# Chunk loads of the first blocks moved into free places of a weight matrix, in a retention kernel with two dense layers

## The chip, the cores and the metric

The kernel runs on one core of a Trainium2 chip. The metric is the device time of one launch in microseconds (us). PE is TensorE, DVE is VectorE, ACT is ScalarE, POOL is GpSimd, SP is the engine whose queue issues nearly all transfers (DMAs).

## The reference

What is computed, shortened (B 4, H 8, S 576, D 64; 2304 tokens, model width 512, hidden width 2048, all in float32):

```python
scores = (1 / sqrt(D)) * q @ k.T                       # per batch and head
Dmat   = where(i >= j, gamma[h] ** (i - j), 0)
x      = ((scores * Dmat) @ v)                         # to [2304, 512]
h      = x @ w_in;  x = (h * cos(h)) @ w_out           # first layer
h      = x @ w_in2                                     # second layer
g      = where(h >= 1, h, where(h <= -1, 0, (h + 1) ** 2 / 4))
out    = g @ w_out2
```

The weights arrive as float64; the kernel takes their words apart and makes of each a pair of float32r numbers (a high and a low part).

## The kernel before

The 2304 tokens are cut into five blocks of 256, 512, 512, 512 and 512 tokens, and a block into chunks of at most 128 tokens of one batch. The first two blocks have seven chunks, called c0 to c6 here (c0 and c1 in the first block, c2 to c6 in the second; c4 and c6 have 64 tokens). The third block has four, called k0 to k3.

**Retention.** A chunk is a `Chunk` object. `load` brings three tensors: `qk` (512 KB), `kv` (512 KB) and `pt`, a table of powers (256 KB for 128 tokens). `prep` multiplies v by a table of powers (one DVE instruction). `scores` puts k times q into two PSUM banks, `masked` multiplies them by the causal mask into the tile R (two DVE instructions), `full` adds the state T times q and forms the new state, `inner` multiplies by R, `state` updates T, and `post` scales the result into `xhl`, the block's input for the first layer as a high and a low part (one ACT and two DVE instructions).

**First layer.** A slot (l, c) is block l with hidden chunk c of 16: `mm1` (12 matmuls into a bank h), then `actA`, `actB`, `actC` on ACT, DVE and POOL (h times cosine, split into `gh` and `gl`), and two slots later `mm2` (12 matmuls into the block's banks). The first two blocks share their weights while these are converted: `slots` interleaves (0, c) with (1, c), block 0 ahead by LEAD. A converted `wi` tile lives in the pool `wr` from its use by (0, c) to its use by (1, c) and is also written to memory (`wd`), to be read again for the later blocks (`load_wi`). The converted `w_out` tiles stay in the places `wo0` to `wo15` of the pool `wp`. Each weight chunk is loaded by `load_raw` into a conversion buffer (`raw` or `rsh` of the pool `cv`, two of each), and `begin` and `convert` work on it with buffers X, W and C of the same pool. From the third slot on, the conversions wait for the last `post` of the first two blocks (`after=lastpost`).

**Second layer.** It starts when the first is done with all blocks; its weights are converted during blocks 2 to 4.

**What sets the order.** The program is written in the order shown, and a list of positions (`plan`, two positions for each slot) places the third block's chunks in the last slots of the second. The tile framework then orders the instructions of every engine by its own timeline and places each tile in its pool; a tile's next user waits until the last one is done. Every engine runs its queue in order. Before, the chunks' `qk` and `kv` share one tile of 16 KB per partition, from the pool `ap` (two places) for even chunks and from `xp` for odd ones. A chunk is asked for when the third before it is done.

Of the kernel before, what the change touches and what calls it, by code (L numbers as in the profile page):

```python
# [7 lines left out]
F32 = mybir.dt.float32  # L8
# [5 lines left out]
AF = mybir.ActivationFunctionType  # L14
# [4 lines left out]
B, H, S, D = 4, 8, 576, 64  # L19
NT, DM, DFF = B * S, H * D, 2048  # L20
P = 128
KB = DM // P
NP = H // 2
NC = DFF // P
# [8 lines left out]
SEQ = {p: k for k, (p, _, _) in enumerate(PRODS)}  # L33
LAG2 = 3
LAG = 2
LEAD = 2
TWICE = 4
MAGIC = 1.5 * 2.0 ** 23
INV2PI = 0.15915494309189535
# [26 lines left out]
def retention_moe_kernel(ctx: ExitStack, tc: tile.TileContext, qk, kv, win1, wout1, win2, wout2, mask, vtab, ptab, out):  # L66
    nc = tc.nc
    V, A, G, SY, PE = nc.vector, nc.scalar, nc.gpsimd, nc.sync, nc.tensor

    const = ctx.enter_context(tc.tile_pool(name="const", bufs=1))  # L70
    wp = ctx.enter_context(tc.tile_pool(name="wp", bufs=1))
    wr = ctx.enter_context(tc.tile_pool(name="wr", bufs=LEAD + 3))
    xp = ctx.enter_context(tc.tile_pool(name="xp", bufs=5))
    ap = ctx.enter_context(tc.tile_pool(name="ap", bufs=2))
    act = ctx.enter_context(tc.tile_pool(name="act", bufs=2))
    stp = ctx.enter_context(tc.tile_pool(name="stp", bufs=4))
    cv = ctx.enter_context(tc.tile_pool(name="cv", bufs=2))
# [83 lines left out]
    wi, wo = {}, {}  # L161
# [80 lines left out]
    CH = {}  # L242
# [8 lines left out]
    class Chunk:  # L251
# [6 lines left out]
            self.first, self.last = self.t == 0, self.t + self.n == S  # L258
            self.banks = banks

        def load(self, other=None, pool=None):
            n = self.n
            both = (pool or ap).tile([P, 4, DM], F32, tag="x" if pool else "qkv", name="qkv")
            self.qk = both[:, 0:2].rearrange("p a (i m) -> p a i m", i=NP)
            self.kv = both[:, 2:4]
            SY.dma_start(out=self.qk, in_=qk[self.i])
            (other or SY).dma_start(out=self.kv[:n], in_=kv[self.i][:n])
            self.pt = ap.tile([P, NP, P], F32, tag="pt", name="pt")
            (other or SY).dma_start(out=self.pt[:, :, :n], in_=ptab[:, :, self.t:self.t + n])

        def prep(self):
            n = self.n
            v = self.kv[:n, 1, :].rearrange("p (h d) -> p h d", h=H)
            V.tensor_tensor(out=v, in0=v, in1=vtb[:n, self.i, :].unsqueeze(2).to_broadcast([n, H, D]), op=ALU.mult)

        def scores(self):
# [4 lines left out]
                    js = slice(j * D, (j + 1) * D)  # L281
                    self.lastpe = PE.matmul(self.Z[j][:n, p * P:p * P + n], self.qk[js, 1, p, :n], self.qk[js, 0, p, :n], start=True, stop=True)

        def masked(self):
            n = self.n
            R = ap.tile([P, 2, NP, P], F32, tag="R", name="R", bufs=1)
            for j in range(2):
                V.tensor_tensor(
                    out=R[:n, j, :, :n], in0=self.Z[j][:n].rearrange("p (i m) -> p i m", i=NP)[:, :, :n],
                    in1=msk[:n, :n].unsqueeze(1).to_broadcast([n, NP, n]), op=ALU.mult)  # L290
            self.R = R

# [46 lines left out]


    slots = []
    for i in range(NC + LEAD):
        if i < NC:
            slots.append((0, i))
        if i >= LEAD:
            slots.append((1, i - LEAD))
    for l in range(2, NBLK):
        slots += [(l, c) for c in range(NC)]
    N1 = len(slots)
# [222 lines left out]
    for l in range(2, NBLK):  # L572
        s0, s1 = window[l]
        span = 2 * (s1 - s0) / len(members[l])
        for k, i in enumerate(members[l]):
            g = int(2 * s0 + k * span)
            e = int(2 * s0 + (k + 1) * span) - 1
            e = max(e, g)
            pos = [g, g + (e - g) // 3, e]
            ends[i] = e  # L580
            gl_ = max(g - 9, ends.get(i - 2, -99))

            banks = (("S", "O"), ("S", "O"), ("y0", "y1"), ("S", "O"))[k] if l == 2 else ("S", "O")

            def mk(i=i, g=g, pos=pos, gl_=gl_, banks=banks):
                def ld():
                    CH[i] = Chunk(i, banks)
                    CH[i].load()
                at(gl_, ld)
                at(g - 1, lambda: CH[i].prep())  # L590
                at(pos[0], lambda: CH[i].scores())
                at(pos[0], lambda: CH[i].masked())
                at(pos[1], lambda: CH[i].full())
                at(pos[1], lambda: CH[i].inner())
                at(pos[1], lambda: CH[i].state())
                at(pos[2], lambda: CH[i].post())
            mk()
# [18 lines left out]
    def first_load(k):  # L616
        i = first[k]
        CH[i] = Chunk(i, (("S", "O"), ("y0", "y1"), ("y2", "y3"))[k % 3])
        if k == 0:
            A.dma_start(out=vtb, in_=vtab)  # L620
            CH[i].load(A)
            A.dma_start(out=msk, in_=mask)
        else:
            CH[i].load(pool=xp if k % 2 else None)

    first_load(0)
    first_load(1)
    load_raw(0, 0, 0)
    first_load(2)
    load_raw(0, 1, 0)  # L630
    CH[first[0]].prep()
    for k, i in enumerate(first):
        c = CH[i]
        c.scores()
        c.masked()
        if k < 2:
            warm(10, c.lastpe)
        if k + 1 < len(first):
            CH[first[k + 1]].prep()
        c.full()  # L640
        c.inner()
        c.state()
        if k < 2:
            warm(10, c.lastpe)
        lastpost = c.post()
        if k + 3 < len(first):
            first_load(k + 3)
        if k == 2:
            make_wi1(0, begin(0, 0, 0))
            load_raw(0, 0, 1)  # L650
        if k == 4:
            make_wo1(0, begin(0, 1, 0))
            load_raw(0, 1, 1)
# [170 lines left out]
```

## Time and profile before

| | us |
|---|---|
| median of three runs (918.47 to 923.39) | 921.04 |
| the profiled execution | 920.45 |
| its span, first to last instruction | 918.6 |
| PE busy, share of the span | 876.8 (95%) |
| DVE busy, share of the span | 635.6 (69%) |
| ACT busy, share of the span | 474.4 (52%) |

A stretch in which PE is busy for its whole length can only be shortened by less work or a higher clock; a stretch in which it is not shows what PE waits for. The granted TensorE clock (PEclk) is given as a share of 2.4 GHz; 0.50 is 1.2 GHz. "A:B" is a stretch in us from the start of the span, "x12" a count of instructions, and "[3.60 <-DMA ...]" the idle time of the engine just before a row and what ended it.

### The profile page before, as it was taken

How to read it: one execution, taken by the hardware profiler on the slowest of the kernel's cores; microseconds unless marked ns; L12 is line 12 of the kernel's file. 1: busy time of each engine (PE TensorE's matmuls, PEld its weight loads, DVE VectorE, ACT ScalarE, POOL GpSimd, SP SyncE). 2: the span in 40 equal slices, each digit the busy share in tenths (PEclk: the TensorE clock that was granted, in tenths of full speed). 3: DMA queues.
4: the chain of work that ended last, by engine and by line, in shares of the span. 5: the costliest groups of instructions: out<-in, count | busy, mean ns of one | idle time of the engine just before them, and what ended most of it. 6: DMA issues, size and time to landing. Idle time of an engine off the chain costs nothing. (4 is left out here: it accounts for less than half of the span.)

```text
span 918.6 us, 13546 instructions
## 1 busy us (share of the span) xinstructions
PE 876.8 (95%) x4876; PEld 752.1 (82%) x4876; DVE 635.6 (69%) x1157; ACT 474.4 (52%) x885; POOL 104.5 (11%) x82
## 2 busy tenths in 40 slices
PE   7878899987999999999999989999899999999997
PEld 6767788876878777788888778888788989889896
DVE  5789899635686786887799787456754556655454
ACT  2348888833565665565677653334433334433332
POOL 0003232300111222222222200000000000000000
PEclk9879999998999999999999999999999999999999
DMA  9869889445487869585976897565575656665531
GB/s 341 274 220 337 292 315 312 161 155 178 161 300 228 307 237 317 178 293 174 322 281 240 296 368 240 178 195 168 201 271 176 190 182 202 221 209 171 166 96 70
DMA packets 78115, 211.81 MB, mean 231 GB/s; under 512 B 9696, under 2 KB 21728, under 8 KB 78048
## 3 DMA queue, kind: packets, MB, share of 16 engines
q1 hardware_dynamic: 77088, 210.01, 68.7%
q10 hardware_dynamic: 960, 0.93, 0.3%
q8 instruction: 39, 0.64, 0.3%
q14 instruction: 28, 0.23, 0.1%
HBM read 170.02 MB, written 40.89 MB: 230 GB/s over the span
## 5 line engine op out<-in xcount | busy, mean ns | idle before, releaser
L493 PE MATMUL hq<-xc,wq 128*128 128x384 f32 x1008 | 200.6, 337 | 5.3 <-ACT sX L508 4.8
L362 PE MATMUL h<-xhl,wi 128*128 128x512 f32 (+1 forms) x864 | 195.5, 374 | 3.7 <-ACT wi L158 2.4
L493 PEld LDWEIGHTS hq<-xc,wq 128*128 128x128 f32 x1008 | 180.1, 188 | 18.9 <-ACT sX L508 5.6
L362 PEld LDWEIGHTS h<-xhl,wi 128*128 128x128 f32 x864 | 151.0, 192 | 32.4 <-ACT wi L158 2.7
L425 POOL TENSOR_TENSOR gl<-t,gh 128x512 fp32r<-128x512 f32 (+1 forms) x78 | 104.3, 1340 | 427.8 <-ACT gh L424 389.5
L424 ACT ACTIVATE gh<-t 128x384 fp32r<-128x384 f32 (+2 forms) x176 | 95.9, 548 | 49.7 <-DVE t L528 27.9
L527 ACT ACTIVATE t<-t,half 128x384 f32<-128x384 f32 x96 | 59.0, 616 | 120.3 <-DVE t L526 120.2
L377 PE MATMUL bky<-gh,wo 128*128 128x512 f32 x256 | 102.6, 401 | 4.1 <-ACT gh L424 4.0
L378 PE MATMUL bky<-gh,wo 128*128 128x512 f32 x256 | 101.2, 395 | 0.0
L379 PE MATMUL bky<-gl,wo 128*128 128x512 f32 x256 | 87.7, 393 | 0.0
L528 DVE TENSOR_TENSOR t<-t,sC 128x384 f32<-128x384 f32 x96 | 53.3, 557 | 35.7 <-ACT t L527 35.7
L545 PE MATMUL bky<-wo,gh 128*128 128x512 f32 x192 | 75.7, 394 | 0.9 <-ACT gh L424 0.9
L546 PE MATMUL bky<-wo,gh 128*128 128x512 f32 x192 | 75.6, 394 | 0.0
L417 ACT ACTIVATE t<-t 128x512 f32<-128x512 f32 (+1 forms) x80 | 46.7, 586 | 52.8 <-DVE t L412 52.4
L425 DVE TENSOR_TENSOR gl<-t,gh 128x384 fp32r<-128x384 f32 (+1 forms) x98 | 54.4, 556 | 19.3 <-ACT gh L424 19.3
L526 DVE TENSOR_SCALAR t<-sC 128x384 f32<-128x384 f32 x96 | 34.3, 358 | 41.5 <-ACT sC L513 40.1
L377 PEld LDWEIGHTS bky<-gh,wo 128*128 128x128 f32 x256 | 48.8, 191 | 16.1 <-ACT gh L424 5.8
L547 PE MATMUL bky<-wo,gl 128*128 128x512 f32 x192 | 61.1, 394 | 0.0
L378 PEld LDWEIGHTS bky<-gh,wo 128*128 128x128 f32 x256 | 48.9, 191 | 9.9 <-issue 0.3
L379 PEld LDWEIGHTS bky<-gl,wo 128*128 128x128 f32 x256 | 48.0, 190 | 10.7 <-POOL gl L425 0.6
L142 DVE SCALAR_TENSOR_TENSOR W<-raw,X 128x512 int32<-128x512 int32 x64 | 52.5, 823 | 1.1
L134 ACT ACTIVATE X<-raw 128x512 f32<-128x512 f32 x64 | 42.3, 663 | 16.5 <-DMA raw<-in_win_dram 11.1
(126 smaller groups left out, 1368.5 us busy)
## 6 DMA issues: line engine op xcount, KB each, us to landing
wq<-wq SPq DMA_DIRECT2D x72, 512.0 KB, 4.1
wi<-wd SPq DMA_DIRECT2D x48, 512.0 KB, 5.0
wo<-wd SPq DMA_DIRECT2D x48, 512.0 KB, 4.6
raw<-in_win_dram SPq DMA_DIRECT2D x32, 512.0 KB, 6.0
raw<-in_wout_dram SPq DMA_DIRECT2D x32, 512.0 KB, 5.7
qkv<-in_qk_dram SPq DMA_DIRECT2D x20, 512.0 KB, 4.5
wd<-wi SPq DMA_DIRECT2D x16, 512.0 KB, 5.2
wd<-cw SPq DMA_DIRECT2D x16, 512.0 KB, 5.7
```

The lines of the kernel that those rows point to most:

```text
L362: PE.matmul(hp[s][:, :n], w[:, a, kb, :], x[b][:, kb, :], start=(i == 0), stop=(i == 3 * KB - 1))
L377: PE.matmul(o, w[:, 0, es], a, start=first and e % per == 0, stop=False, skip_group_check=True)
L378: PE.matmul(o, w[:, 1, es], a, start=False, stop=False, skip_group_check=True)
L379: PE.matmul(o, w[:, 0, es], b, start=False, stop=last, skip_group_check=True)
L424: A.activation(a, u, AF.Copy)
L425: eng.tensor_tensor(out=b, in0=u, in1=f(a), op=ALU.subtract)
L493: PE.matmul(o, w[:, a, kb, :], x[b][:, kb, :], start=first and i == 0, stop=i == 5, skip_group_check=True)
L527: A.activation(t, t, AF.Square, scale=0.5, bias=half)
L528: V.tensor_tensor(out=t, in0=t, in1=h, op=ALU.max)
L545: PE.matmul(y, a[:, js], w[:, 0, :], start=n == 0, stop=False)
L546: PE.matmul(y, a[:, js], w[:, 1, :], start=False, stop=False)
L547: PE.matmul(y, b[:, js], w[:, 0, :], start=False, stop=n == NC - 1)
```

## The change

`load` takes a list of homes: a place for `qk`, one for `kv` and one for `pt`. Chunks c2 to c6 get their places among `wo3` to `wo15`, which hold nothing yet, and c0 and c1 keep `ap`. All seven chunks are asked for ahead of the first `scores`. R alternates between its old tile and `wo2`. In the second block, `prep` becomes eight ACT instructions of 64 columns. LEAD grows to 3, `wr` keeps five tiles, and `slots` lets block 0 lead by one slot at first, by two from slot 6 and by three from slot 10. The third block's chunks k0 to k3 all use the banks S and O (k2 had y0 and y1), and k2 and k3 are loaded into conversion buffers (`raw`, `rsh` and C) as soon as the last weights of the first layer have left them.

```diff
-LEAD = 2
+LEAD = 3
...
-    wr = ctx.enter_context(tc.tile_pool(name="wr", bufs=LEAD + 3))
+    wr = ctx.enter_context(tc.tile_pool(name="wr", bufs=LEAD + 2))
...
-        def load(self, other=None, pool=None):
+        def load(self, other=None, homes=None):
+
             n = self.n
-            both = (pool or ap).tile([P, 4, DM], F32, tag="x" if pool else "qkv", name="qkv")
...
+            if homes is None:
+                both = ap.tile([P, 4, DM], F32, tag="qkv", name="qkv")
+                self.qk, self.kv = both[:, 0:2], both[:, 2:4]
+                self.pt = ap.tile([P, NP, P], F32, tag="pt", name="pt")
+            else:
+                self.qk, self.kv = [p_.tile([P, 2, DM], F32, tag=g_, name="qkv") for p_, g_ in homes[:2]]
+                self.pt = homes[2][0].tile([P, NP, P], F32, tag=homes[2][1], name="pt")
...
             v = self.kv[:n, 1, :].rearrange("p (h d) -> p h d", h=H)
+            if self.blk == 1:
+                for h in range(H):
+                    A.activation(v[:, h, :], v[:, h, :], AF.Copy, scale=vtb[:n, self.i, h:h + 1])
+                return
             V.tensor_tensor(out=v, in0=v, in1=vtb[:n, self.i, :].unsqueeze(2).to_broadcast([n, H, D]), op=ALU.mult)
...
-    for i in range(NC + LEAD):
-        if i < NC:
-            slots.append((0, i))
-        if i >= LEAD:
-            slots.append((1, i - LEAD))
+
+    n0 = 0
+    for i in range(NC):
+        while n0 < min(NC, i + (2 if i < 6 else 3 if i < 10 else LEAD + 1)):
+            slots.append((0, n0))
+            n0 += 1
+        slots.append((1, i))
...
-            banks = (("S", "O"), ("S", "O"), ("y0", "y1"), ("S", "O"))[k] if l == 2 else ("S", "O")
...
+            if l == 2:
+
+                gl_ = 2 * s0 - 9
+                if k >= 2:
+                    gl_ = 2 * pos_of[0, NC - 1] + 2
+                    homes = (cv, "raw"), (cv, "rsh"), (cv, "C")
...
-            CH[i].load(pool=xp if k % 2 else None)
+
+            CH[i].load(homes=None if k == 1 else ((wp, f"wo{19 - 2 * k}"), (wp, f"wo{18 - 2 * k}"), (wp, f"wo{k + 1}") if k < 5 else (ap, "pt")))
...
-    first_load(2)
+    for k in range(2, 5):
+        first_load(k)
     load_raw(0, 1, 0)
+    for k in range(5, len(first)):
+        first_load(k)
+    load_raw(0, 0, 1)
...
-        c.masked()
+        c.masked((None, "wo2")[k % 2])
...
-        if k + 3 < len(first):
-            first_load(k + 3)
```

How this moves instructions, on three engines. Line numbers of the changed kernel are its own.

SP's queue in the start, before. `qkv_410` is c6, `qkv_350` c5, `qkv_1918` the third block's k0; `raw` is a weight chunk on its way to conversion.

```order
L266 DMA qkv_410<-in_qk_dram 128x1024
L267 DMA qkv_410<-in_kv_dram 64x1024
L269 DMA pt_306<-in_ptab_dram 128x4x64
L266 DMA qkv_350<-in_qk_dram 128x1024
L267 DMA qkv_350<-in_kv_dram 128x1024
L269 DMA pt_353<-in_ptab_dram 128x4x128
L266 DMA qkv_1918<-in_qk_dram 128x1024
L267 DMA qkv_1918<-in_kv_dram 128x1024
```

SP's queue in the start, with the change. `qkv_193` and `qkv_194` are c5, `qkv_199` and `qkv_200` c6, `qkv_1920` is k0.

```order
L272 DMA qkv_193<-in_qk_dram 128x1024
L273 DMA qkv_194<-in_kv_dram 128x1024
L272 DMA qkv_199<-in_qk_dram 128x1024
L273 DMA qkv_200<-in_kv_dram 64x1024
L118 DMA raw_205<-in_win1_dram 128x1024
L118 DMA raw_490<-in_wout1_dram 128x1024
L118 DMA raw_587<-in_win1_dram 128x1024
L272 DMA qkv_1920<-in_qk_dram 128x1024
L273 DMA qkv_1920<-in_kv_dram 128x1024
```

The pair for c5 and c6 was the 22nd to 26th row of SP's queue, behind rows that wait for buffers; now it is the 16th to 19th, with only loads into free places ahead of it.

ACT's queue in the start, before (T is c0's state, `xhl` a chunk's `post`, X, wi and wo the conversions):

```order
L134 ACTIVATE X<-raw 128x512
L323 ACTIVATE T<-bkS 64x4x64 x2
L158 ACTIVATE wi<-W 128x512
L134 ACTIVATE X<-raw 128x512
L337 ACTIVATE xhl<-xs 128x4x128
L134 ACTIVATE X<-raw 128x512
```

ACT's queue in the start, with the change; the rows on `vtb` are `prep` of c2, c3, c4, c5 and c6:

```order
L335 ACTIVATE T<-bkS 64x4x64 x2
L281 ACTIVATE qkv<-qkv,vtb 128x64 x8
L158 ACTIVATE wi<-W 128x512
L349 ACTIVATE xhl<-xs 128x4x128
L281 ACTIVATE qkv<-qkv,vtb 128x64 x8
L281 ACTIVATE qkv<-qkv,vtb 64x64 x8
L349 ACTIVATE xhl<-xs 128x4x128
L134 ACTIVATE X<-raw 128x512
L281 ACTIVATE qkv<-qkv,vtb 128x64 x8
L158 ACTIVATE wo_481<-W 128x512
L281 ACTIVATE qkv<-qkv,vtb 64x64 x8
L349 ACTIVATE xhl<-xs 128x4x128
```

The `xhl` of c1 now stands behind the `prep` of c3 and c4, and that of c2 behind the `prep` of c5 and c6, each of which waits for its own `kv`.

PE's queue in the third block's retention, before (`qkv_1937` is k1, `qkv_2230` k3, R the masked scores; the eight `scores` rows of k3 are followed by the `mm2` of the last two slots of block 1):

```order
L282 MATMUL bkO_2191<-qkv_1937 128x128 x4
L304 MATMUL bkS_2190<-qkv_1937 64x64 x8
L299 MATMUL bkO_2191<-qkv_1937,T_90 128x128 x4
L312 MATMUL bkO_2191<-R_2200,qkv_1937 64x128 x8
L282 MATMUL bkS_2316<-qkv_2230 128x128
L282 MATMUL bkO_2317<-qkv_2230 128x128
```

PE's queue at the same place with the change (`qkv_1925` is k1, `qkv_2080` k2, `h_2365` the `mm1` of slot (1, 15), `bky` the `mm2` of slot (1, 13)):

```order
L316 MATMUL bkS_2197<-qkv_1925 64x64 x8
L376 MATMUL h_2365<-xhl_377,wi_1907 128x512 x4
L376 MATMUL h_2365<-xhl_378,wi_1907 128x512 x4
L376 MATMUL h_2365<-xhl_377,wi_1907 128x512 x4
L311 MATMUL bkO_2198<-qkv_1925,T_90 128x128 x4
L324 MATMUL bkO_2198<-R_2207,qkv_1925 64x128 x8
L291 MATMUL bkS_2283<-qkv_2080 128x128 x4
L291 MATMUL bkO_2284<-qkv_2080 128x128 x4
L391 MATMUL bky0_814<-gh_2273,wo13_1854 128x512
```

A slot of block 1, first `mm1` and then `mm2`, now stands between the chunks, and k2 comes ahead of k3.

## Rows read from the trace of the kernel before

**Rows 1.** Busy time of each engine, granted clock and DMA share by stretch.

```profile
11.50:53.80 42.30, 33.96 (x388) 29.92 (x389) 33.06 (x65) 14.40 (x30) 1.46 (x2) 0.81 0.82 267
53.80:57.70 3.90, 1.54 (x9) 1.25 (x7) 3.90 (x9) 1.42 (x4) 0.00 (x0) 0.50 0.90 317
57.70:204.90 147.20, 138.13 (x820) 119.72 (x820) 118.35 (x211) 110.78 (x231) 35.57 (x28) 0.98 0.77 266
204.90:228.30 23.40, 16.90 (x128) 14.02 (x128) 13.04 (x22) 7.18 (x13) 0.00 (x0) 0.85 0.46 158
```

Columns: the stretch and its length, then PE, PEld, DVE, ACT and POOL, the clock, the share of the DMA engines' time, GB/s.

**Rows 2.** What DVE waited for in 11.5 to 53.8: us in total, times, longest.

```profile
DVE qkv L274 <- DMA qkv<-in_kv_dram: 3.0, 3, 2.3
DVE T L325 <- PE bkO L299: 2.4, 2, 1.6
DVE xhl L338 <- ACT xhl L337: 1.7, 3, 0.7
```

**Rows 3.** Timeline of the first stage: start, length, engine, line, operation.

```profile
11.52 0.69 DVE L288 TENSOR_TENSOR R<-bkS,msk 128x512 f32<-128x512 f32 x1 [1.74 <-DMA msk<-in_mask_dram]
42.43 0.79 SPq L267 DMA_DIRECT2D qkv<-in_kv_dram  x1
47.94 0.69 DVE L274 TENSOR_TENSOR qkv<-qkv,vtb 128x512 f32<-128x512 f32 x1 [2.26 <-DMA qkv<-in_kv_dram]
53.36 0.43 DVE L338 TENSOR_TENSOR xhl<-xs,xhl 128x256 fp32r<-128x256 f32 x1 [0.48 <-ACT xhl L337]
57.66 5.68 PE L362 MATMUL h<-xhl,wi 128*128 128x256 f32 x20 [2.36 <-ACT wi L158]
```

**Rows 4.** The `prep` instructions alone in the same stretch: length, DVE busy.

```profile
11.50:53.80 42.30, 4.11 (x6) 0.81 0.82 267
```

**Rows 5.** Timeline, ACT: its smallest and a mid-sized instruction.

```profile
2.47 0.20 ACT L601 ACTIVATE half<-half 128x1 f32<-128x1 f32 x1
38.07 0.42 ACT L410 ACTIVATE t<-hs 128x256 f32<-128x256 f32 x1
```

**Rows 6.** Start, by stretch: length, clock, DMA share, GB/s.

```profile
0.00:10.00 10.00, 1.00 0.84 281
10.00:20.00 10.00, 0.83 1.03 405
20.00:30.00 10.00, 0.86 1.06 342
```

**Rows 7.** What PE waited for in 57.7 to 204.

```profile
PE bky L377 <- ACT gh L424: 4.0, 2, 2.6
PE bkS L377 <- ACT gh L424: 3.1, 1, 3.1
```

**Rows 8.** Timeline at the third block's retention, SP, DVE and PE.

```profile
203.80 1.09 PE L312 MATMUL bkO<-R,qkv 128*64 128x128 f32 x16
204.83 0.69 DVE L274 TENSOR_TENSOR qkv<-qkv,vtb 128x512 f32<-128x512 f32 x1 [2.17 <-DMA qkv<-in_kv_dram]
204.93 0.34 SPq L266 DMA_DIRECT2D qkv<-in_qk_dram  x1
208.50 0.55 PE L282 MATMUL bkS<-qkv 64*128 64x128 f32 x1 [3.60 <-DMA qkv<-in_qk_dram]
213.66 0.63 PE L378 MATMUL bky<-gh,wo 128*128 128x512 f32 x1
215.44 0.39 PE L377 MATMUL bky<-gh,wo 128*128 128x512 f32 x1
```

**Rows 9.** Timeline of the last slots: an `mm1` of block 1, and that of (0, 15).

```profile
175.79 0.52 PE L362 MATMUL h<-xhl,wi 128*128 128x256 f32 x3
189.95 2.91 PE L362 MATMUL h<-xhl,wi 128*128 128x512 f32 x12
```

**Rows 10.** The converted `wi`, DVE's last step: times, first and last start.

```profile
L159 DVE SCALAR_TENSOR_TENSOR wi<-C,X x14: 677/692/1040, 58.7 to 162.0; 128x512 fp32r<-128x512 int32 x14
```

**Rows 11.** DMA issues of the whole run: KB each, us to landing.

```profile
raw<-in_wout_dram SPq DMA_DIRECT2D x32, 512.0 KB, 5.7
```

More of the change, by code (lines that the diff above doesn't have):

```diff
@@ L259, in __init__ @@
             self.banks = banks
-        def load(self, other=None, pool=None):
+        def load(self, other=None, homes=None):
             n = self.n
-            both = (pool or ap).tile([P, 4, DM], F32, tag="x" if pool else "qkv", name="qkv")
-            self.qk = both[:, 0:2].rearrange("p a (i m) -> p a i m", i=NP)
-            self.kv = both[:, 2:4]
+            if homes is None:
[5 more added lines that the diff above has]
+                self.pt = homes[2][0].tile([P, NP, P], F32, tag=homes[2][1], name="pt")
+            self.qk = self.qk.rearrange("p a (i m) -> p a i m", i=NP)
             SY.dma_start(out=self.qk, in_=qk[self.i])
             (other or SY).dma_start(out=self.kv[:n], in_=kv[self.i][:n])
-            self.pt = ap.tile([P, NP, P], F32, tag="pt", name="pt")
             (other or SY).dma_start(out=self.pt[:, :, :n], in_=ptab[:, :, self.t:self.t + n])
@@ L282, in scores, with masked @@
                     self.lastpe = PE.matmul(self.Z[j][:n, p * P:p * P + n], self.qk[js, 1, p, :n], self.qk[js, 0, p, :n], start=True, stop=True)
-        def masked(self):
+        def masked(self, home=None):
             n = self.n
-            R = ap.tile([P, 2, NP, P], F32, tag="R", name="R", bufs=1)
+            if home is None:
+                R = ap.tile([P, 2, NP, P], F32, tag="R", name="R", bufs=1)
+            else:
+                R = wp.tile([P, 2, NP, P], F32, tag=home, name="R")
             for j in range(2):
@@ L581, in retention_moe_kernel, with mk @@
             gl_ = max(g - 9, ends.get(i - 2, -99))
-            banks = (("S", "O"), ("S", "O"), ("y0", "y1"), ("S", "O"))[k] if l == 2 else ("S", "O")
-            def mk(i=i, g=g, pos=pos, gl_=gl_, banks=banks):
+            homes = None
+            if l == 2:
[3 more added lines that the diff above has]
+                    homes = (cv, "raw"), (cv, "rsh"), (cv, "C")
+            def mk(i=i, g=g, pos=pos, gl_=gl_, homes=homes):
                 def ld():
-                    CH[i] = Chunk(i, banks)
-                    CH[i].load()
+                    CH[i] = Chunk(i)
+                    CH[i].load(homes=homes)
                 at(gl_, ld)
@@ L645, in retention_moe_kernel @@
         lastpost = c.post()
-        if k + 3 < len(first):
-            first_load(k + 3)
         if k == 2:
             make_wi1(0, begin(0, 0, 0))
-            load_raw(0, 0, 1)
         if k == 4:
```

## The prediction

> **What bounds the kernel now.** I read the page first: PE is busy 95% of the span, so a gain can only come from stretches where PE stands idle or runs at the lower of its two clock levels. The stretches by engine [rows 1] show where these are. From 57.7 us to 204.9 PE is busy 138.13 of 147.20 us at a mean clock of 0.98: 9.07 us idle in all. Ahead of it lies the first stage, the retention of c0 to c6, which ends with the last `post` at 53.36 + 0.43 = 53.79 us [rows 3]. Its clock is 0.81, PE is busy 33.96 and DVE 33.06 of 42.30 us, so neither is full; the two hand work to each other. Behind it comes a gap of 3.90 us in which PE does 1.54 us of work, since the conversions of the third `wi` wait for the last `post`; PE starts on it at 57.66, after 2.36 us of idle time [rows 3]. The last weak stretch is the third block's retention, 204.90 to 228.30: PE busy 16.90, idle 6.50 us. From 228 us on I expect nothing to move but the start.
>
> What DVE waits for in the first stage [rows 2]: 3.0 us on a chunk's `kv`, the longest 2.26 us at 47.94, and 2.4 and 1.7 us on PE and ACT, with some smaller ones. The wait at 47.94 is for the third block's k0: its `kv` was issued only at 42.43 [rows 3], because its place was taken until then, and its `prep` stands in DVE's queue ahead of the `post` of c5.
>
> In the third block [rows 8], SP issues k3's `qk` at 204.93, after k1's last matmuls (from 203.80, 1.09 us long) have freed the place. PE waits for it from 204.90 to 208.50 (3.60 us), with the `mm2` of two slots queued behind. After it PE runs at the lower level: successive matmuls of 512 columns take 0.63 us at 213.66, and 0.39 at 215.44.
>
> **Part 1, the first stage.** (a) Loads ahead. All 14 `qk` and `kv` come without waiting for a chunk to end. The transfers are near their limit in this stage: 342 to 405 GB/s at a share above 1.0 from 10 to 30 us [rows 6]. The seven chunks and the first two raw weights are about 9.2 MB (c0 to c3 1.31 MB each, c4 0.92, c5 and c6 without their `pt` 1.05 and 0.79, two raw weights 1.05, the small tables 0.15). The first 10 us brought 2.8 MB, the next 4.05, so the rest, 2.35 MB, is in 6 to 7 us later, at about 27 us. DVE needs c6 some ten us after that. The waits for `kv` go: −3.0 us. That cover is gone only if the loads take more than about ten us longer.
>
> (b) `prep` on ACT. DVE loses four of the six `prep` instructions that it has in this stretch (five go, and k1's comes in from behind it), at 4.11/6 = 0.69 us each [rows 4]: 2.7 us; and one instruction of 256 columns (0.4 us, the length of the row at 53.36) moves behind the stretch: −3.1 us in all. On ACT the trace has no instruction of 64 columns. Its bounds are the 0.20 us of one column and the 0.42 us of 256 [rows 5]; I take 0.26, a quarter of the way, which is nearer the small one in columns. Eight make 2.1 us a chunk (1.6 to 3.4), 10.5 us for five chunks, and ACT, busy 14.40 of 42.30 us, has room. But ACT runs in order: the `xhl` of c1 and c2 now stand behind the `prep` of c4 and c6, thus behind their `kv`, which land at about 20 and 27 us. DVE reaches the last step of these two `post` at about 21 and 30 us by a count of its instructions from 11.52, at 0.6 us for 512 columns and 0.35 for less. With 2.1 us of `prep` and 0.6 of `xhl` the first is late by some 1.5 us and the second is not late. I charge +1.0 (0 to 13: at the upper price, 3.4 against 0.69 us, with nothing hidden, five chunks cost 2.7 us more each).
>
> The Trainium skill speaks against this edit: its page "ScalarE: Activation LUTs", section "Rules for kernel authors", wants multiplications on VectorE. The section "What ACT_TABLE_LOAD costs" gives 186 ns and 0.833 ns a column, and 93 ns more for a scale read from a tile; by it, as an estimate, one instruction takes 0.33 us and a chunk 2.7, and the sum below would be about 1 us worse. By 186 + 213 ns a row of 256 columns is 0.40 us, and the trace's 0.42 agrees.
>
> (c) Sum of the stage: DVE's work 33.06 − 3.1 = 29.9; its idle time 42.30 − 33.06 = 9.24, less 3.0, is 6.2 (the hand-over between PE, DVE and ACT stays as it is); with 1.0 it is 37.1 against 42.30: −5.1 us (0 to −9; −9 if half of the hand-over goes too).
>
> (d) The wait at 57.66. The conversion still starts with the last `post`. But with a lead of one slot PE's queue has slot (1, 0) there, whose `mm1` needs no new weight: 2.91 us by the row of such twelve matmuls [rows 9] at the higher clock. It covers the 2.36 us: −2.4 (0 to −2.4). Part 1 is −7.5.
>
> **Part 2, the first layer of the first two blocks.** The same instructions, in another interleaving. Early, each `wi` is needed one slot of block 1 later than before; from slot 10 one earlier. Before, the last `wi` was finished by DVE at 162.0 us [rows 10] and first used near 175.8 [rows 9], 13.8 us ahead; a slot of block 1 is about 5.4 us of PE work (two times twelve matmuls of 0.225, the spacing within the 2.91). So the later need is covered. The waits for `gh` (7.1 us [rows 7]) come from the chain of ACT and DVE, and nothing here shortens it. I take 0 (−3 to +5).
>
> **Part 3, the third block.** k2 and k3 are loaded while the last slots of block 1 run, into buffers that the conversion leaves at about 162 to 170 us, 30 us before PE needs them. The 3.60 us go. So does, I expect, the half speed behind them: from 208.50 to 215.44 PE needs 6.94 us for what takes 3.47 at the higher level. What is late next is the hand-over through R and T, which makes up the other 6.50 − 3.60 = 2.9 us; slot (1, 15) and the `mm2` of (1, 13) now lie between the chunks, so it shouldn't grow. Against it: the raw weights of the second layer take the buffers only after k2 and k3, behind the stores of block 1's result on SP, and their first conversion step stands in DVE's queue just ahead of k3's last `post` step. A raw load needs 5.7 us to land [rows 11]; DVE gets there about 4 us after PE's last `mm2`, and PE has about 5 us of other chunks to do. And the `kv` of k3 stands on SP behind a reload of `wi` that waits for PE, so its `prep` may hold DVE for 2 us like the one at 204.83 [rows 8]. I charge +1.0 for both (0 to +7). Part 3: −3.60 − 3.47 + 1.0 = −6.1.
>
> **Sum.** −7.5 + 0 − 6.1 = −13.6. The profiled execution took 920.45, 0.6 below the median of 921.04, so I forecast 907.
>
> **The rivals.** What a measurement of this kernel can tell from no change is about 0.5%, 4.6 us.
>
> R2, only the first stage gains: a load on DVE's queue or the hand-over takes back part 3. For it: DVE waited 2.17 us for a `kv` at 204.83 too, and what feeds the last `mm2` runs through DVE. Against it: the `mm1` between the chunks. 920.45 − 7.5 = 913.
>
> R3, only the third block gains: ScalarE becomes what paces the first stage, at the upper price of 13 us less what part 1 gives. That is the mechanism of the multiplications on ACT; it decides from about 2.2 us a chunk beyond DVE's 0.69, with nothing hidden. Against it: ACT's idle time. 920.45 − 6.1 = 914; at the full 13 us it is 920.
>
> The rule of the Trainium skill on multiplications ("ScalarE: Activation LUTs", "Rules for kernel authors") is this rival.
>
> R4, the change doesn't do what it says: the start is bound by the transfers, whose share is above 1.0, and earlier requests land no earlier; and PE's wait at 204.9 only turns into one for `gh`, since the `gh` of slot (1, 14) was late there too. Against it: the share falls below 1 after 30 us, while the stage lasts to 53.8. 920.
>
> R5, slower: with a lead of three, four of the five `wi` tiles are in use between (0, c) and (1, c), and ACT and DVE can write the next only when `mm1` of (1, c − 5) is done. Its place is the last four weights; before, two places were spare. Each has about 8 us of PE work between the release and the use. It decides if the conversion, queued in order, comes more than 3.4 us too late each time (4 × 3.4 eats the 13.6); at a whole slot of block 1, 5.4 us, it is +21.6: 920.45 − 13.6 + 21.6 = 928. Against it: the 13.8 us of advance.
>
> **How the numbers follow.** Forecast 0.62 (its own range 900 to 913), R2 0.13, R3 0.09, R4 0.09, R5 0.07. The likeliest is 907. The range 897 to 916 takes the better bounds of parts 1 and 2 (−4 and −3) below, and R2 and R3 above; it leaves out R4, R5 and little else. Faster by over 0.5% (below 916.4): the forecast whole (0.62), R2 (0.12 of 0.13) and R3 in most of its span (0.07): 0.81. R4 and the rest: 0.12. Slower: 0.07.
>
> **What would show it.** In the profile after: the last `post` of c6 ends near 49 us instead of 53.8, without a wait of DVE for `kv` in the stage; ACT has forty short rows of about 0.26 us; PE goes from the last chunk into (1, 0) with no gap of 2 us; from there to block 1's end PE's idle time is still about 9 us, and there is no wait of ACT for PE before `wi`; k3's `scores` come without waiting for a DMA, the clock stays at 1.0 there, and the third block's first `mm1` starts about 14 us earlier than 228.3. Wrong would be: the first stage ending after 52 us with ACT full in it; the clock at half level for longer while PE starts on the first slots; or a new wait for `gh` in the slots of block 1 once the lead is three.

## The result, and the profile after

The changed kernel takes 907.27 us (median of four runs, 905.65 to 907.96) where the kernel before takes 921.22 beside it: a ratio of 0.9848, interval 0.9818 to 0.9877, so 14.0 us less. The forecast was 907. The profiled execution took 905.65, its span 903.8 us; PE is busy 97% of it.

Four stretches show where the time came from. Their bounds are points at which PE has the same work behind it in both kernels: the end of the last `post` of the first stage (there to within three short matmuls); the point at which `mm2` of (1, 12) has ended, with `mm1` of (1, 15), the last three `mm2` of block 1 and the third block's chunks still to come; and the first `mm1` of the third block.

| stretch | before, us | after, us | difference |
|---|---|---|---|
| to the end of the first stage's last `post` | 53.79 | 48.67 | −5.1 |
| from there to 189.95 [rows 9], after 181.87 | 136.16 | 133.20 | −3.0 |
| the third block's retention, to 228.34, after 212.73 | 38.39 | 30.86 | −7.5 |
| from there to the end of the span | 690.3 | 691.1 | +0.8 |

The stretches by engine of the changed kernel (start and end, length, then PE, PEld, DVE, ACT and POOL, the clock, the share of the DMA engines, GB/s) answer to [rows 1]:

```profile
11.50:48.70 37.20, 31.27 (x391) 27.96 (x392) 30.26 (x60) 22.82 (x67) 1.01 (x1) 0.83 0.95 330
53.80:181.90 128.10, 121.30 (x672) 104.14 (x672) 111.62 (x197) 102.01 (x218) 37.22 (x28) 0.99 0.86 292
181.90:212.70 30.80, 30.57 (x265) 25.63 (x264) 20.61 (x33) 14.57 (x26) 1.27 (x1) 1.00 0.60 206
```

The first stage is shorter by five microseconds, but its PE clock is as low as before (0.83), and DVE still stands idle for 6.9 of 37.2 us. In the third block PE is busy for all but 0.2 us, at the full clock.

What DVE waits for in the first stage after the change (us in all, times, longest) answers to [rows 2]:

```profile
DVE C L152 <- DMA raw<-in_wout_dram: 4.4, 1, 4.4
DVE xhl L350 <- ACT xhl L349: 1.8, 3, 0.9
DVE R L300 <- DMA msk<-in_mask_dram: 1.5, 1, 1.5
DVE R L300 <- PE bky L291: 0.2, 1, 0.2
```

The waits for `kv` are gone, and those for T on PE too. But the waits for `kv` went with `prep` to ACT, whose row in the same view is

```profile
ACT qkv L281 <- DMA qkv<-in_kv_dram: 7.4, 5, 2.5
```

In DVE's queue stands a wait that the kernel before does not have: a conversion step waits 4.4 us for the first raw `w_out`, which on SP's queue now stands behind the loads of c2 to c4.

The timeline of the same kernel (start, length, engine, line, operation) gives the places that answer to [rows 3] and [rows 8]:

```profile
19.67 2.02 ACT L281 ACTIVATE qkv<-qkv,vtb 128x64 f32<-128x64 f32 x8 [1.44 <-DMA qkv<-in_kv_dram]
48.24 0.43 DVE L350 TENSOR_TENSOR xhl<-xs,xhl 128x256 fp32r<-128x256 f32 x1 [0.15 <-ACT xhl L349]
49.37 3.21 PE L376 MATMUL h<-xhl,wi 128*128 128x512 f32 x12
53.78 3.97 PE L376 MATMUL h<-xhl,wi 128*128 128x256 f32 x20 [1.21 <-ACT wi L158]
79.58 0.39 PE L391 MATMUL bkS<-gh,wo 128*128 128x256 f32 x1 [2.75 <-ACT gh L438]
189.19 3.06 PE L376 MATMUL h<-xhl,wi 128*128 128x512 f32 x12
198.99 1.16 PE L291 MATMUL bkS<-qkv 64*128 64x128 f32 x8
212.73 2.14 PE L376 MATMUL h<-xhl,wi 128*128 128x512 f32 x8
```

A chunk's `prep` takes 2.02 us on ACT; slot (1, 0) runs at 49.37, ahead of the slot that needs the third `wi`; twenty matmuls of that slot take 3.97 us, where they took 5.68 at the lower clock; the wait for `gh` of [rows 7] is still there, 2.75 us at 79.58; `mm1` of (1, 15) lies between two chunks at 189.19, and k3's scores start at 198.99 without a wait. This much looks like the prediction. The experiments show that it is not the same as its reasons.

### The profile page after: what moved, and what is told of

The parts are those of the page before. It is cut to its first block, busy times and chain, and to the rows that moved or that the text cites. A ratio compares the mean times of both kernels' runs of the same rounds, so it can differ in the third digit from the quotient of the medians.

```text
span 903.8 us, 13583 instructions
## 1 busy us (share of the span) xinstructions
PE 874.5 (97%) x4876; PEld 750.3 (83%) x4876; DVE 633.2 (70%) x1152; ACT 482.1 (53%) x925; POOL 107.0 (12%) x82
## 4 chain that ended last, share of the span: by engine, by line
PE 64%; DVE 14%; DMA 7%; ACT 6%; issue 4%; SPq 0%; DVEq 0%; ACTq 0%
PE hq L507 18%; PE h L376 10%; PE bky L559 5%; PE bky L560 5%; PE bky L561 5%; PE bky L391 3%; PE bky L392 3%; PE bky L393 3%; DVE W L142 2%; DMA raw<-in_wout_dram 2%; DVE t L426 2%; DMA raw<-in_win_dram 2%; DMA wi<-wd 1%; DVE X L141 1%; DVE t L446 1%
## 5 line engine op out<-in xcount | busy, mean ns | idle before, releaser
L439 POOL TENSOR_TENSOR gl<-t,gh 128x512 fp32r<-128x512 f32 (+1 forms) x78 | 106.8, 1370 | 409.6 <-ACT gh L438 379.9
L142 DVE SCALAR_TENSOR_TENSOR W<-raw,X 128x512 int32<-128x512 int32 x64 | 48.8, 762 | 1.1
```

The lines of the kernel that those rows point to most:

```text
L142: V.scalar_tensor_tensor(out=Wi, in0=hi, scalar=-0x80000000, in1=Xi, op0=ALU.bitwise_and, op1=ALU.bitwise_or)
L439: eng.tensor_tensor(out=b, in0=u, in1=f(a), op=ALU.subtract)
```

## The experiments

All times are medians; the kernel before, on the same chip each time, took 920.5 in the first four runs, 920.7 in the next four and 922.1 in the last four. A difference between two profiles alone can be chance: over two profiles of the changed kernel the first `mm1` of the third block starts at 212.73 and 213.87. And a profiled execution can lie some us from its kernel's median: that of prep_on_vector took 901.03, its fastest, that of three_edits_together 905.61, its slowest. The table gives for each run the time, the ratio to before with its interval, the end of the first stage's last `post`, and that first `mm1`.

| run | us | ratio to before | last `post` ends | first `mm1`, block 3 |
|---|---|---|---|---|
| third_old_places | 906.6 | 0.9839 (0.9813 to 0.9865) | 47.4 | 212.0 |
| first_loads_old | 907.6 | 0.9864 (0.9840 to 0.9889) | 51.0 | 214.3 |
| lead_two_at_start | 907.1 | 0.9858 (0.9832 to 0.9883) | 49.3 | 214.7 |
| raw_wout_earlier | 907.0 | 0.9845 (0.9823 to 0.9867) | 46.8 | 212.4 |
| first_stage_alone | 916.6 | 0.9952 (0.9933 to 0.9971) | 48.8 | 224.0 |
| lead_and_third_alone | 909.3 | 0.9869 (0.9849 to 0.9890) | 55.4 | 217.8 |
| third_two_slots | 911.8 | 0.9897 (0.9870 to 0.9924) | 49.7 | 219.3 |
| prep_on_vector | 905.4 | 0.9821 (0.9797 to 0.9846) | 49.9 | 210.8 |
| early_loads_lead_two | 915.1 | 0.9934 (0.9912 to 0.9957) | 49.3 | 221.3 |
| one_place_for_R | 904.2 | 0.9809 (0.9787 to 0.9831) | 50.5 | 212.7 |
| changed_again | 906.4 | 0.9836 (0.9808 to 0.9864) | 49.3 | 213.9 |
| three_edits_together | 903.1 | 0.9796 (0.9770 to 0.9821) | 49.5 | 211.8 |

**One part undone at a time.** The first four runs undo or shift one part each.

third_old_places: k2 and k3 of the third block go back to the old places and the old time of loading.

```diff
-            if l == 2:
-
+            if l == 2 and k < 2:
                 gl_ = 2 * s0 - 9
-                if k >= 2:
-                    gl_ = 2 * pos_of[0, NC - 1] + 2
-                    homes = (cv, "raw"), (cv, "rsh"), (cv, "C")
```

> The changed kernel, but the third block's last two chunks k2 and k3 are loaded as before the change (into the two places of the pool ap, when k0 and k1 have left them); their banks stay S and O and the lead stays. By the forecast (the early load is worth the 3.6 us wait and the half speed behind it): 6 to 7.5 us slower than the changed kernel, 913 to 915, with a wait of TensorE for the qk of k3 and a drop of the granted clock near 200 us. By the rival (the slot of block 1 that now lies between the chunks hides the load anyway): 0 to 2 us slower, 907 to 909, no such wait.

It measured 906.6: nothing lost. My theory, that the early load is the gain, falls. The trace of this kernel shows why:

```profile
193.46 0.33 SPq L272 DMA_DIRECT2D qkv<-in_qk_dram  x1
195.30 0.50 PE L391 MATMUL bky<-gh,wo 128*128 128x512 f32 x1
197.24 1.07 PE L393 MATMUL bky<-gl,wo 128*128 128x512 f32 x4
198.24 0.93 PE L291 MATMUL bkS<-qkv 64*128 64x128 f32 x6
```

The `qk` of k3 is asked for as late as in the kernel before, after k1's last matmuls, and k3's scores still come without a wait: the scores of k2 and the `mm2` of a slot fill the 4.8 us from 193.46 to 198.24. In the kernel before the same load took from 204.93 to 208.50 [rows 8], with nothing of PE's beside it.

first_loads_old: the chunks c2 to c6 go to their old places, and a load is asked for when a chunk ends; the second raw `wi` also comes behind the third chunk, as before.

```diff
-            CH[i].load(homes=None if k == 1 else ((wp, f"wo{19 - 2 * k}"), ...
+            CH[i].load(pool=xp if k % 2 else None)
...
         lastpost = c.post()
+        if k + 3 < len(first):
+            first_load(k + 3)
```

> The changed kernel, but chunks c2 to c6 are loaded into the old places at the old pace (asked for when the third chunk before is done); prep on ScalarE, the lead and the third block stay as changed. By the forecast (the loads ahead carry the first stage's gain): last post near 52 to 54 us instead of 48.7, 4 to 6 us slower, 911 to 913. By the rival (what gained was prep off VectorE and slot (1, 0) ahead of (0, 2)): last post near 49 to 50 us, 0 to 2 us slower, 907 to 909.

The stage ends 2.3 us later, but the time is the same within the interval: DVE waits for T on PE instead (4.9 us in two waits) and no longer for the raw `w_out`.

lead_two_at_start: block 0 leads by two slots from the start, so that (1, 0) comes behind the slot that needs the third `wi`.

```diff
-        while n0 < min(NC, i + (2 if i < 6 else 3 if i < 10 else LEAD + 1)):
+        while n0 < min(NC, i + (3 if i < 10 else LEAD + 1)):
```

> The changed kernel, but block 0 leads by two slots from the start (as before the change) and by three from slot 10, so slot (0, 2) with its new weight stands ahead of (1, 0). By the forecast (the mm1 of (1, 0) covers the wait for the third wi, 2.4 us; the trace after adds that the clock came back to full there, some 2.6 us more): TensorE waits 2 to 4 us for wi before (0, 2) and the clock stays at half behind it, 2.4 to 5 us slower, 910 to 912. By the rival (the wait only moves to the next weights, TensorE has to wait for the conversions in any order): same, 907 to 908.

The wait is there, and so is the lower clock, as this kernel's timeline shows:

```profile
53.14 6.35 PE L376 MATMUL h<-xhl,wi 128*128 128x256 f32 x20 [3.74 <-ACT wi L158]
```

That is 2.5 us more of waiting and 2.4 us more for the same matmuls than in the changed kernel (53.78, above), yet the time is 907.1. The slots that follow give most of it back: the third block begins at 183.45, against 181.96 and 183.13 in the two profiles of the changed kernel.

raw_wout_earlier: the first raw `w_out` is asked for ahead of c3 and c4.

```diff
-    for k in range(2, 5):
-        first_load(k)
+    first_load(2)
     load_raw(0, 1, 0)
+    for k in range(3, 5):
+        first_load(k)
```

> The changed kernel, but the first raw w_out is asked for ahead of c3 instead of behind c4. In the trace after, VectorE waits 4.4 us for it at 25.7 us. If that wait sets the first stage: last post 2 to 4 us earlier (45 to 46.5 us), 903.5 to 905.5. If the stage hangs on the transfers as a whole (c5 and c6 land later by as much) : last post stays near 48.7, 907.

The 4.4 us wait goes, and the stage ends 1.8 us earlier. But PE then waits 4.67 us for a `gl`, and the time stays at 907.0:

```profile
69.71 2.02 PE L393 MATMUL bky<-gl,wo 128*128 128x512 f32 x4 [4.67 <-POOL gl L439]
```

**The change in halves.** Undoing one part shows little, so the next two runs take the change apart at its middle.

first_stage_alone keeps the first stage, and takes lead, slots and the third block from the kernel before.

```diff
-LEAD = 3
+LEAD = 2
...
-            n0 += 1
-        slots.append((1, i))
+        if i >= LEAD:
+            slots.append((1, i - LEAD))
```

> The first stage as in the changed kernel (all loads ahead in free places, second place for R, prep on ScalarE); the lead, the order of the slots and the third block as before. Theory (two gains that add up: the first stage, and the third block's chunks lying over three slots instead of two): 920.5 - 7 = 913, range 911 to 915, last post at 48 to 49 us, first mm1 of the third block 6 to 8 us earlier than 228.3, its wait for k3's qk still there. Rival 1 (each half alone gives nearly all, since waits behind it absorb the rest): 908 to 910. Rival 2 (the slots behind the stage give its gain back, as they did in the runs before): 917 to 921.

lead_and_third_alone is the other half: the loads as in first_loads_old, and besides

```diff
-            if self.blk == 1:
-                for h in range(H):
-                    A.activation(v[:, h, :], v[:, h, :], AF.Copy, scale=vtb[:n, self.i, h:h + 1])
-                return
...
-        c.masked((None, "wo2")[k % 2])
+        c.masked()
```

> The other half: lead, order of slots and third block as changed; the first stage wholly as before (old places and pace, one place for R, prep on VectorE). Theory: 920.5 - 7.5 for the third block and up to 2.4 for slot (1, 0) ahead of the third weight = 911 to 913; last post at 53 to 54 us, no stall of PE over 0.5 us between 180 and 230 us. Rival 1 (each half alone gives nearly all): 908 to 910. Rival 2 (the first stage's gain is given back, so this half is the whole gain): 906 to 909.

The first stage alone is worth 4.1 us and the other half 11.4; together they would be 15.5, and the change measures 14.0 and 15.7 in its two sets of runs. At the first `mm1` of the third block it is 4.4 and 10.5 us, and 15.6 together (14.5 in the second profile). Within this spread the halves add up; neither contains the other. Both times lie outside what I had as theory (911 to 915, and 911 to 913): the first stage is worth less, and the other half more. Of the 10.5 us 2.9 come before the third block, which begins at 187.09 where the point of the same work was 189.95, and 7.6 in it.

The timeline of lead_and_third_alone, and its stretches behind the first of these rows, with the columns of the stretches above:

```profile
50.00 1.12 PE L312 MATMUL bkS<-qkv 64*64 64x64 f32 x16 [1.82 <-DVE R L296]
55.02 0.42 DVE L346 TENSOR_TENSOR xhl<-xs,xhl 128x256 fp32r<-128x256 f32 x1 [0.48 <-ACT xhl L345]
217.82 2.14 PE L372 MATMUL h<-xhl,wi 128*128 128x512 f32 x8
```

```profile
50.00:60.00 10.00, 10.00 (x61) 8.95 (x62) 7.22 (x16) 3.09 (x6) 0.00 (x0) 0.53 0.55 163
...
58.00:59.00 1.00, 1.00 (x4) 0.76 (x3) 1.00 (x3) 0.36 (x1) 0.00 (x0) 0.50 0.95 306
59.00:60.00 1.00, 1.00 (x5) 0.82 (x4) 1.00 (x3) 0.87 (x2) 0.00 (x0) 0.75 0.57 116
60.00:62.00 2.00, 2.00 (x16) 1.84 (x15) 2.00 (x6) 0.99 (x2) 0.00 (x0) 1.00 0.91 260
```

The last `post` is 1.6 us later than in the kernel before, yet PE has no gap from 50 to 62 us, because `mm1` of (1, 0) lies in its queue ahead of the slot that needs the third `wi`. The wait of 2.36 us [rows 3] is gone, as (d) had it.

**The third block.** third_two_slots keeps everything, but plans the third block's four chunks over the last two slots of block 1, as before.

```diff
-    window = {2: (b1_end - LEAD + 1, b1_end + 1)}
+    window = {2: (b1_end - 1, b1_end + 1)}
```

> As changed, but the third block's four chunks are planned over the last two slots of block 1 as before, not over three. Theory (the matmuls of the slot that lies between the chunks are the cover): 912 to 915, and PE stands idle 3 to 7 us more between 180 and 230 us. Rival (the early loads are the cover, or the order of the mm2 alone is enough): 906 to 908.

early_loads_lead_two is the counterpart: lead, slots and the two-slot window as before, the first stage as changed, and the early loads of k2 and k3. Beside first_stage_alone it differs by these loads, and by k2's scores, which use the banks S and O as in the changed kernel and not y0 and y1:

```diff
+                gl_ = 2 * s0 - 9
+                if k >= 2:
+                    gl_ = 2 * pos_of[0, NC - 1] + 2
+                    homes = (cv, "raw"), (cv, "rsh"), (cv, "C")
```

> The first stage and the early loads of k2 and k3 as changed, but the lead, the order of the slots and the two-slot window of the third block as before; beside it stands the run with the first stage alone (916.6). It is the early loads where they were meant to act. My prediction's step (the load is what PE waits for): the 3.75 us of idle time and the half clock behind it go, 6 to 7 us less than 916.6, 909.5 to 911. Rival (the hand-over between PE and VectorE ends at the same time as the load and takes its place; the matmuls between the chunks are the cover): 914 to 917, with as much idle time of PE between 180 and 225 us.

Without the third slot the changed kernel loses 4.5 us (6.6 at the first `mm1`), though k2 and k3 are loaded early; against the changed kernel's second set of runs it is 5.4. From 180 to 230 us PE stands idle for 3.8 us, where it is 0.4 in the changed kernel. A row of its timeline and one of its stretches show the wait and the lower clock:

```profile
199.78 1.13 PE L291 MATMUL bkS<-qkv 64*128 64x128 f32 x8 [2.14 <-issue]
```

```profile
190.00:210.00 20.00, 16.83 (x131) 14.34 (x132) 11.66 (x20) 7.76 (x14) 0.00 (x0) 0.83 0.41 132
```

The early loads, with the banks of k2, gain 1.5 us on first_stage_alone by the medians, with overlapping intervals, and 2.9 by what each is below the kernel before beside it (2.7 at the first `mm1`). I had 6 to 7. The timeline of early_loads_lead_two shows what took their place:

```profile
154.85 0.33 SPq L273 DMA_DIRECT2D qkv<-in_kv_dram  x1
157.72 0.38 SPq L273 DMA_DIRECT2D qkv<-in_kv_dram  x1
195.69 0.42 SPq L273 DMA_DIRECT2D qkv<-in_kv_dram  x1
200.63 0.69 DVE L283 TENSOR_TENSOR qkv<-qkv,vtb 128x512 f32<-128x512 f32 x1 [2.36 <-DMA qkv<-in_kv_dram]
202.28 0.43 DVE L337 TENSOR_TENSOR T<-bkS,T 64x256 f32<-64x256 f32 x1
202.81 1.70 PE L291 MATMUL bkS<-qkv 64*128 64x128 f32 x8 [2.30 <-issue]
```

The `kv` of k2 and k3 are there from about 160 us on. But the two old places are now free for the next block's chunks, and the `prep` of the first of these stands in DVE's queue in the middle of the third block. It waits 2.36 us for a `kv` that was issued at 195.69, the update of T stands behind it, and PE's next scores, which write the bank that the update reads, start as it ends (the profile names no releaser, "issue"; the two times show it). In first_stage_alone, without early loads, DVE waits 2.37 us at the same place for k2's own `kv`. A load moved away from there brings the next one forward.

The hand-over was late in the kernel before too. There PE's wait of 3.60 us ends at 208.50 with the `qk` of k3 [rows 8]. But k3's scores also need the bank O of k1, and DVE, held by the `kv` at 204.83, had read it only at 207.65 + 0.69 = 208.34: with k3's `qk` there, PE would still have waited for all but 0.2 us of it. In first_stage_alone the wait at the same place, 3.75 us, is put down to this very step of DVE. A row of the timeline of the kernel before, and one of first_stage_alone:

```profile
207.65 0.69 DVE L330 TENSOR_TENSOR xs<-bkO,pt 128x512 f32<-128x512 f32 x1
```

```profile
204.68 0.55 PE L291 MATMUL bkS<-qkv 64*128 64x128 f32 x1 [3.75 <-DVE xs L342]
```

**The parts of the first stage.** prep_on_vector leaves out the branch for block 1 in `prep` (first piece of the diff of lead_and_third_alone); one_place_for_R is its second piece.

> As changed, but prep of block 1 back on VectorE. Theory (VectorE's work sets the first stage's end): last post later by 2 to 3.5 us, time 909 to 911. Rival 1 (VectorE waits for a transfer in the stage anyway, 4.4 us for a raw w_out, which takes up the 2.8 us): last post within 1 us of 48.7, time 906 to 908. Rival 2 (ScalarE's eight short instructions held up what stood behind them): 904 to 906.

> As changed, but R of the first stage has one place again. Theory (the second place lets masked of a chunk run while PE still reads the R before it; with it the waits of VectorE and PE for T and R in the stage went): last post 1 to 3 us later than 48.7, first mm1 of the third block 1 to 3 us later than 212.7, time 907 to 909. Rival (the place is not needed, since the loads and prep took the waits away): last post within 0.5 us of 48.7, 906 to 908.

Neither part is needed for the time. With `prep` on DVE the time is 905.4, with one place for R 904.2; the changed kernel, run again beside the latter, is at 906.4. In both the last `post` ends later than in the changed kernel (by 1.2 and 1.8 us of its 48.67, or 0.6 and 1.2 of the 49.31 of its second profile), and the first `mm1` of the third block does not. What DVE waits for in the first stage of prep_on_vector shows where the extra work went:

```profile
DVE qkv L279 <- DMA qkv<-in_kv_dram: 2.8, 2, 2.3
DVE R L296 <- DMA msk<-in_mask_dram: 1.5, 1, 1.5
DVE xhl L346 <- ACT xhl L345: 0.8, 2, 0.7
DVE t L422 <- ACT t L421: 0.6, 1, 0.6
```

The 4.4 us wait for the raw `w_out` is gone, and 2.8 us of waiting for `kv` are back, though all loads are ahead. DVE works 33.66 us up to the last `post` where it was 30.26, and stands idle 4.7 us where it was 6.9: two thirds of the added work lie in time in which it otherwise stood idle. Its wait for `xhl` on ACT falls from 1.8 to 0.8 us, so rival 2 may hold as well; the times do not tell the two apart. The Trainium skill's page "ScalarE: Activation LUTs", section "Rules for kernel authors", wants multiplications on VectorE; these runs bear that out in so far as moving them away gained nothing.

changed_again is the changed kernel without an edit, and three_edits_together puts together prep_on_vector, third_old_places and raw_wout_earlier.

> The changed kernel itself once more, beside the next one: 905 to 909 by every theory; the spread of first mm1 of the third block (212.7 before) over two profiles tells how much of a difference of 1 us there is chance.

> As changed, with the three edits that came out no slower put together: prep back on VectorE, k2 and k3 of the third block loaded to the old places at the old time, the first raw w_out asked for ahead of the chunks c3 and c4. If what each spared in the profile adds up (2 us of the first mm1 of the third block for prep, 0.7 for the old places, 0.3 for the raw w_out): 903 to 905, first mm1 of the third block at 209 to 211. If they are one and the same slack, or chance: 905 to 908.

903.1 us is the lowest time of the study: 3.3 us under the changed kernel beside it. The two intervals (0.9770 to 0.9821, and 0.9808 to 0.9864) overlap, so it is likely but not settled that it beats the changed kernel. It does beat the kernel before, by 2.0%. The time lies where I expected it if the gains of the three edits add up, the first `mm1` of the third block, at 211.8, where I expected it if they are one and the same slack. The profile is that of its slowest execution, so which of the two holds stays open.

## Why the prediction was right, and where its reasons were not

**What bounds the kernel.** Right. All of the gain lies in the weak stretches ahead of 228.3, and behind it nothing moved by more than 0.8 us.

**Sum of the first stage, (c).** The last `post` ended 5.1 us earlier, for a forecast of 5.1. In time, the stage alone is worth 4.1 us. That the two 5.1 agree is luck, since the terms do not. I had −3.0 for DVE's `kv` waits (a), −3.1 for its work (b), +1.0 for ACT, and nothing for the hand-over. In the run DVE's work fell by 2.8 us (33.06 to 30.26) and its idle time by 2.3 (9.24 to 6.94): its `kv` waits went, its waits for PE and ACT shrank from 5.9 us (with the small ones that [rows 2] leaves out) to 2.0, and 4.4 us for the raw `w_out` came in. So the step that failed is "the hand-over between PE, DVE and ACT stays as it is", and the sum lacked the raw weight. The reason for (a) failed too: with all loads ahead and `prep` on DVE, in prep_on_vector, DVE still waits 2.8 us for `kv`; in the changed kernel these waits stand on ACT. And the worth of (b) was mis-sized: without it the stage ends 0.6 to 1.2 us later, not 3.1, and the time does not grow. I had seen that SP's queue was filled with all loads ahead, but counted only when the chunks land, not when the raw weight behind them does. The second place for R I did not price at all; in one_place_for_R the time does without it. Which part of the first stage gives its 4.1 us stays open: with the loads, `prep` or R taken back one at a time, nothing is lost.

**Price of `prep` on ACT.** I took 2.1 us a chunk, and the row shows 2.02. The Trainium skill's "ScalarE: Activation LUTs", section "What ACT_TABLE_LOAD costs", gave 0.33 us for one instruction as an estimate, and I made 2.7 of eight. A grouped row of the changed kernel (busy, then mean ns of one) agrees on the one and not on the eight:

```profile
L281 ACT ACTIVATE qkv<-qkv,vtb 128x64 f32<-128x64 f32 x24 | 6.1, 335 | 4.6 <-DMA qkv<-in_kv_dram 4.6
```

One takes 335 ns, but three times eight are busy for 6.1 us: they overlap, and follow each other about every (2.02 − 0.335) / 7 = 0.24 us. The same section of the Trainium skill says that ACTIVATEs back to back overlap by about 93 ns, which I had left out. With it the estimate for eight is 0.33 + 7 × 0.24 = 2.0 us, and the trace's 2.02 agrees.

**The wait at 57.66, (d).** Mechanism right, value in the total not. (1, 0) covers the start of the slots, and the lower clock goes too, which I had not counted: [rows 3] has 5.68 us for twenty matmuls, and it is 3.97 after. But lead_two_at_start takes the cover away, loses 4.9 us at this place, and the time does not move. The slots behind it give most of it back. The same happened with raw_wout_earlier. In that stretch DVE is busy 111.62 of 128.10 us in the changed kernel; I think that its conversions set the pace at which PE can use up a head start there, but no run here tells that apart.

**Part 2.** I took 0. From the end of the first stage to the point just ahead of the third block it is −3.0 us (−2.4 in the second profile), where I had the −2.4 of (d). Lead and slots bring it without the changed first stage as well (187.09 to set against 189.95). How it divides between the start and the later slots stays open: without the start's order, in lead_two_at_start, the third block begins 1.5 us later than in the first profile and 0.3 later than in the second.

**Part 3.** Forecast −6.1, measured −7.5, for another reason. The step that failed is "k2 and k3 are loaded while the last slots of block 1 run ... The 3.60 us go". The load and the hand-over ended within 0.2 us of each other, at 208.50 and 208.34, and I read the wait as the load's alone. With the early loads and the old window only 1.5 us go (2.9 by the other count); with the new window and the old loads all of the gain stays. I had named the cause in half a sentence, the matmuls "between the chunks", as the reason why the hand-over would not grow. It is the main thing: a window of three slots, whose width LEAD sets, puts a slot's `mm1` and `mm2` between the chunks, and they cover the load, the hand-over through R and T and the next `prep`, all of them, so that PE is idle for only 0.2 us and the clock stays at 1.0. Whether such a window needs the lead of three, and what the banks of k2 add, no run shows. Of the 2.9 us that I put to the hand-over, 0.69 were a wait for the next block's `qk` at 226.73. What I had charged 1.0 for, a `prep` that holds DVE for a `kv`, came for the next block's first chunk instead, 0.99 us at 191.75 in the changed kernel; behind the cover it costs nothing.

**The rivals.** R2 (only the first stage gains, 913) and R3 (only the third block, 914) name a time for one half alone; the halves measured 916.6 and 909.3, and the change is about their sum. R2's mechanism, a load in DVE's queue that takes back part 3, is there without the third slot (early_loads_lead_two). R3's is not: ACT is busy 22.82 of 37.20 us in the stage. R4's mechanism, that the wait for the load only turns into another, is what early_loads_lead_two shows; it did not decide because the slots were spread as well. R5's waits did not come: between 48.7 and 182 us ACT waits ahead of `wi` only for DVE (4.7 us), and DVE begins the last `wi` at 162.4 us, where it was 162.0 [rows 10].

**The sum.** I had −13.6 and the medians give −14.0, the two profiles −14.8. That it came so close is luck in part: in the first stage what I had put at nothing and what I had left out nearly cancel, and in the third block the gain came by another way than the one I had priced. The lower end of the range does not come out of its terms: 907 − 4 − 3 is 900, not 897.

## What to carry to other kernels

A wait that the profile names can be the last of several that end close together, here 0.2 us apart: before a load is moved to remove it, ask what ends next there, and prefer an edit that puts independent work of the waiting engine into the gap, since that covers all of them at once. Undoing one part at a time can show part after part as worthless while the whole is worth 14 us; splitting the change into two halves told more here. And time saved at one place is counted only from a later point at which both kernels have done the same work, because the stretch between can give it back, as it did with most of the 4.9 us of lead_two_at_start.

## What the runs showed of the hardware that was not expected

In lead_and_third_alone PE is busy without a gap from 50 us on, and still its clock stays at the lower level until 59 us; only from 60 on is it at 1.00 (the stretches from 50 to 62 us above). Up to 54.06 this work is the last chunk's retention, then `mm2` and `mm1`. Before 50 us the clock was low already; PE had waited for 0.83 us up to 45.35 and for 1.82 us up to 50.00. In the changed kernel the clock is low too around the end of the stage, after a wait of 1.12 us up to 46.67, but only until 50 us:

```profile
48.00:50.00 2.00, 2.00 (x10) 1.90 (x9) 1.85 (x6) 1.97 (x5) 0.00 (x0) 0.51 0.32 82
50.00:52.00 2.00, 2.00 (x10) 1.61 (x10) 2.00 (x5) 0.15 (x1) 0.00 (x0) 1.00 0.20 58
```

So the cost of a low clock was paid behind the waits as well, in one run through nine microseconds of unbroken work, in the other through some three. Why the two differ, no run here shows.
